# Contracting the first layer of the x tokens over (head, slot) instead of over channels, with M = state @ w_in built on the chip and all stages pipelined anew

## The chip, the cores and the metric

The kernel runs on one core of one Trainium2 chip. The time is the device time of one execution in microseconds (us). A profile is a trace of one execution; its span is about 1.8 us shorter than the time of the same execution.

The engines are called as the profile calls them: PE is TensorE (PEld its weight loads, which overlap its matmuls), DVE is VectorE, ACT is ScalarE, POOL is GpSimd, SP is SyncE. PEclk is the TensorE clock that the profile reports as granted (1.00 is full). The kernels' tiles lie in two on-chip memories: every matmul here writes a PSUM tile, and all other tiles are in SBUF.

## The reference, cut to what matters

Two blocks follow each other. The first is a cross attention in both directions between 512 tokens and 32 state slots for each of 8 batches and 8 heads of 64 channels. The second is a feed-forward block over all 4352 resulting tokens (8 x 512 "x tokens" and 8 x 32 "state tokens").

```python
B, H, S, Ns, D = 8, 8, 512, 32, 64          # d_model = H*D = 512, d_ff = 2048
# attention, per batch and head (scores are scaled by 1/sqrt(D))
a      = softmax(x @ state.T)               # 512 x 32: over the slots
xread  = a @ state                          # 512 x 64
a2     = softmax(state @ x.T)               # 32 x 512: over the tokens
sread  = a2 @ x                             # 32 x 64
t = concat([xread, sread]) over tokens, heads side by side   # (B*544) x 512
# feed-forward
h = t @ w_in                                # 512 -> 2048
g = s * relu(h)**2 + b                      # s and b are single numbers
out = g @ w_out                             # 2048 -> 512
```

The change rests on one identity. For the x tokens, h = sum over the heads of (a_head @ state_head) @ w_in_head = sum over the heads of a_head @ (state_head @ w_in_head). The bracket is M. The left form contracts over 512 channels, and the right form over 8 heads x 32 slots = 256.

## The kernel before

Almost all that PE reads is in fp16. In the transposed layout a batch is a 128x512 tile for every 128 rows of the contraction. The attention builds U = xread.T from the attention weights (`a4`, with 4 heads x 32 slots on the partitions). ACT casts U to the fp16 tiles `XB`, which the first layer reads:

```python
def attn_phase2b(b, ctx):                    # a4 = E * (1 / its sum over slots)
    for g in range(NG):                      # 2 groups of 4 heads
        RBG = ps_tile([P, S], FP32, ...)
        mm(RBG, ind16, R4h_g[g], tp=(0, 0))  # spread the reciprocals by a matmul
        nc.vector.tensor_mul(a4, E4_g[g], RBG)

def attn_phase2cd(b, ctx):
    ...                                      # sread of the batch into srdT (V)
    for g in range(NG):
        for pp in range(2):
            for m in range(2):               # U: contraction over 32 slots
                mm(U[64*m:64*m+64, :], stN[32*hp:32*hp+32, :],
                   a4[32*hp:32*hp+32, :], tp=(32*hp, 64*m))
            nc.scalar.copy(xb, U)            # xb is XB: 4 tiles of 128 channels

def moe_mm1(rhs_tiles, ntok, tag, frange):
    for f in frange:                         # 16 chunks of 128 of d_ff
        for k in range(NKM):                 # 4 matmuls: 512 channels
            nc.tensor.matmul(hps, w_in16[k][:, P*f:P*f+P], rhs_tiles[k], ...)
        nc.scalar.activation(r16, hps, AF.Relu)
        nc.vector.tensor_mul(gt, r16, r16)

def moe_mm2(gts, ntok, out_aps, tag):
    for rr in range(ntok // P):
        for f in range(NKF):                 # 16 matmuls: 2048
            nc.tensor.matmul(ops, gts[f][:, P*rr:P*rr+P], w_out16[f], ...)
        nc.vector.scalar_tensor_tensor(osb, ops, s_bc, bias_bc, ALU.mult, ALU.add)
        nc.sync.dma_start(out_aps[rr], osb)

for b in range(B):
    ...                                      # loads for b + 1
    ctx_b = attn_phase1_2a(b)
    if b > 0: gts_prev = moe_mm1(XB of b-1, chunks 0..7)
    if b == 1: ...                           # 16 matmuls: column sums of w_out, for b
    attn_phase2b(b, ctx_b)
    if b > 0: gts_prev += moe_mm1(XB of b-1, chunks 8..15)
    attn_phase2cd(b, ctx_b)
    if b > 0: moe_mm2(gts_prev, ...)         # all four token groups in a row
```

The second layer is applied to relu(h)^2 alone; s and b come in at the eviction, where `bias_bc` is b times the column sums of w_out.

The softmax here doesn't subtract the row's maximum and nothing guards it: scores larger than these inputs give would overflow.

## Time and profile before

| | before |
|---|---|
| time, median of 4 runs | 319.28 us (319.2 to 320.52) |
| profiled span | 317.4 us |
| PE busy | 297.0 us, 94% |
| DVE, ACT busy | 41%, 35% |
| length of one steady batch | 33.94 us |

The page of the kernel before begins with the busy time of each engine, its share and its number of instructions. Its second part shows tenths of PE's time in 40 equal slices, and its fourth the shares of the chain of work that ended last.

```profile
span 317.4 us, 4788 instructions
PE 297.0 (94%) x1889; PEld 137.8 (43%) x1889; DVE 130.7 (41%) x348; ACT 110.2 (35%) x209; POOL 71.8 (23%) x114
PE   1698799999999999999999999999999999999990
...
PE 87%; DMA 5%; POOL 5%; issue 0%; DVE 0%; POOLq 0%
```

PE works without a visible gap from the sixth slice to the last but one. An average could hide a stage with another limit, so look at stretches of one batch. In the windows of the kernel before, the columns are the stretch and its length, then the busy time and number of instructions of each engine.

```profile
core 0: us, PE busy (x) PEld busy (x) DVE busy (x) ACT busy (x) POOL busy (x), PEclk, DMA share, GB/s
65.30:99.24 33.94, 33.94 (x224) 15.52 (x222) 15.27 (x43) 12.88 (x24) 7.57 (x12) 1.00 0.36 49
167.10:201.00 33.90, 33.90 (x224) 15.50 (x222) 15.22 (x42) 12.88 (x24) 7.36 (x11) 1.00 0.37 50
```

In a steady batch PE is busy for the whole stretch, and the two engines after it less than half of it. Only PE work counts there. What that work is, the chain of waits of the kernel before shows (start, length, what):

```profile
72.41 0.86 PE hps_x_4_924 L282 x4
...
84.04 0.33 PE U_0_0_1080 L67 x2
84.38 0.01 PE U_0_1_1085 L67 x2
84.38 0.21 PE U_1_0_1090 L67 x2
84.59 0.02 PE U_1_1_1095 L67 x2
84.61 3.56 PE ops_x_0_1100 L300 x16
88.17 3.45 PE ops_x_1_1120 L300 x16
```

Four first-layer matmuls take 0.86 us and sixteen second-layer matmuls 3.45 us, so one 128x512 matmul costs 0.216 us of PE, called a slot below. A batch has 64 of each: 128 x 0.216 = 27.6 us. The remaining 6.3 us are attention. The four matmuls of each U group, which use parts of the PE array, cost about one slot together: 0.33 + 0.01 for the first, 0.21 + 0.02 for the second.

### The profile page before, as it was taken

To read this page: it belongs to the slowest core of one execution; us is meant where nothing else is said; L and a number is where in the kernel's file an instruction comes from. 1 tells how busy PE (TensorE), PEld (TensorE's weight loads), DVE (VectorE), ACT (ScalarE), POOL (GpSimd) and SP (SyncE) were. 2 spreads that over 40 slices of the span, in tenths; PEclk is the share of its full clock that TensorE was granted. 3 is DMA by queue.
4 is the path that set the end of the run, shared out by engine and by line. 5 is a ranking of instruction groups with operands and counts; after the bars stand their busy time and mean duration, and the time that the engine had idled before them with its cause. 6 is when DMAs were issued, how large, how long until landed. Compare 5 with 4: busy or idle time off the path is not lost.

```text
span 317.4 us, 4788 instructions
## 1 busy us (share of the span) xinstructions
PE 297.0 (94%) x1889; PEld 137.8 (43%) x1889; DVE 130.7 (41%) x348; ACT 110.2 (35%) x209; POOL 71.8 (23%) x114
## 2 busy tenths in 40 slices
PE   1698799999999999999999999999999999999990
PEld 0343344444444444444444444444444444466440
DVE  0434345156324651266227532564146622554110
ACT  1126223035602561056304650357015620674000
POOL 8728964300350007000800053000000000000000
PEclk9999799999999999999999999999999999999997
DMA  7999993910292009300671039100110001000211
GB/s 47 160 207 188 91 74 26 143 40 1 15 124 72 0 0 98 97 16 0 57 115 37 3 22 114 68 0 2 66 66 3 0 35 66 33 3 0 90 48 63
DMA packets 46489, 18.18 MB, mean 57 GB/s; under 512 B 39554, under 2 KB 41602, under 8 KB 46466
## 3 DMA queue, kind: packets, MB, share of 16 engines
q0 software_dynamic: 41152, 8.92, 31.1%
q1 hardware_dynamic: 5314, 8.95, 8.0%
q8 instruction: 15, 0.25, 0.3%
q14 instruction: 8, 0.07, 0.1%
HBM read 17.86 MB, written 8.91 MB: 84 GB/s over the span
## 4 chain that ended last, share of the span: by engine, by line
PE 87%; DMA 5%; POOL 5%; issue 0%; DVE 0%; POOLq 0%
DMA w_out_0_129<-in_moe_w_out_dram 4%; POOL xn_0_112 L120 2%; PE ops_x_0_693 L300 1%; PE ops_x_0_3121 L300 1%; PE ops_x_0_2728 L300 1%; PE ops_x_0_2321 L300 1%; PE ops_x_0_1100 L300 1%; PE ops_x_0_1914 L300 1%; PE ops_x_0_1507 L300 1%; PE cs_ps L329 1%; DMA stH_1_164<-in_state_dram 1%; PE ops_sr_3589 L300 1%; PE ops_x_2_3529 L300 1%; PE ops_x_0_3489 L300 1%; PE ops_x_3_3181 L300 1%; PE ops_x_1_2748 L300 1%
## 5 line engine op out<-in xcount | busy, mean ns | idle before, releaser
L282 PEld LDWEIGHTS <-w_in_0_121 128*128 128x128 f16 x144 | 14.2, 98 | 16.7 <-issue 4.0
L282 PEld LDWEIGHTS <-w_in_3_127 128*128 128x128 f16 x144 | 14.2, 99 | 14.5 <-issue 1.3
L282 PEld LDWEIGHTS <-w_in_2_125 128*128 128x128 f16 x144 | 14.2, 99 | 12.8 <-issue 0.6
L282 PEld LDWEIGHTS <-w_in_1_123 128*128 128x128 f16 x144 | 14.2, 99 | 12.7 <-issue 1.0
L120 POOL DMA_DIRECT2D xn_6_1999<-in_x_dram x8 | 5.9, 747 | 18.7 <-PE Vps_1_1_1884 L67 18.7
L120 POOL DMA_DIRECT2D xn_7_2406<-in_x_dram x8 | 5.9, 746 | 18.7 <-PE Vps_1_1_2291 L67 18.7
L120 POOL DMA_DIRECT2D xn_4_1185<-in_x_dram x8 | 5.9, 746 | 18.7 <-PE Vps_1_1_1070 L67 18.7
L120 POOL DMA_DIRECT2D xn_5_1592<-in_x_dram x8 | 5.9, 746 | 18.7 <-PE Vps_1_1_1477 L67 18.7
L120 POOL DMA_DIRECT2D xn_3_778<-in_x_dram x8 | 5.9, 746 | 6.8 <-PE Vps_1_1_663 L67 6.7
L120 POOL DMA_DIRECT2D xn_2_349<-in_x_dram x8 | 5.9, 746 | 0.0
L120 POOL DMA_DIRECT2D xn_1_166<-in_x_dram x8 | 5.9, 745 | 0.0
L120 POOL DMA_DIRECT2D xn_0_112<-in_x_dram x8 | 5.9, 745 | 0.0
L290 ACT ACTIVATE r_x_0_2521<-hps_x_0_2516 128x512 f16<-128x512 f32 x1 | 0.6, 598 | 13.7 <-PE hps_x_0_2516 L282 13.7
L290 ACT ACTIVATE r_x_0_1707<-hps_x_0_1702 128x512 f16<-128x512 f32 x1 | 0.6, 598 | 13.7 <-PE hps_x_0_1702 L282 13.7
L290 ACT ACTIVATE r_x_0_1300<-hps_x_0_1295 128x512 f16<-128x512 f32 x1 | 0.6, 597 | 13.7 <-PE hps_x_0_1295 L282 13.7
L290 ACT ACTIVATE r_x_0_2114<-hps_x_0_2109 128x512 f16<-128x512 f32 x1 | 0.6, 597 | 13.7 <-PE hps_x_0_2109 L282 13.7
L290 ACT ACTIVATE r_x_0_2914<-hps_x_0_2909 128x512 f16<-128x512 f32 x1 | 0.6, 597 | 13.7 <-PE hps_x_0_2909 L282 13.7
L67 PE MATMUL stTps_175<-ident_91,stH_0_110 32*128 32x32 f16 x4 | 0.3, 188 | 5.3 <-DMA stH_0_110<-in_state_dram 5.3
L290 ACT ACTIVATE r_x_0_3206<-hps_x_0_3201 128x512 f16<-128x512 f32 x1 | 0.6, 597 | 13.0 <-PE hps_x_0_3201 L282 13.0
L67 PEld LDWEIGHTS <-xn_0_112 128*64 128x64 f16 (+1 forms) x48 | 2.3, 143 | 5.6 <-issue 3.6
L290 ACT ACTIVATE r_x_0_893<-hps_x_0_888 128x512 f16<-128x512 f32 x1 | 0.6, 598 | 12.0 <-PE hps_x_0_888 L282 12.0
L199 ACT ACTIVATE E_0_0_201<-T_0_0_196 128x512 f16<-128x512 f32 x1 | 0.6, 597 | 8.9 <-PE T_0_0_196 L67 8.9
(2153 smaller groups left out, 868.1 us busy)
## 6 DMA issues: line engine op xcount, KB each, us to landing
xn_0_112<-in_x_dram POOLq DMA_DIRECT2D x8, 64.0 KB, 2.9
w_in_0_121<-in_moe_w_in_dram POOLq DMA_DIRECT2D x1, 512.0 KB, 5.4
w_in_1_123<-in_moe_w_in_dram POOLq DMA_DIRECT2D x1, 512.0 KB, 7.4
w_in_2_125<-in_moe_w_in_dram POOLq DMA_DIRECT2D x1, 512.0 KB, 9.3
w_in_3_127<-in_moe_w_in_dram POOLq DMA_DIRECT2D x1, 512.0 KB, 11.2
xn_1_166<-in_x_dram POOLq DMA_DIRECT2D x8, 64.0 KB, 3.0
xn_2_349<-in_x_dram POOLq DMA_DIRECT2D x8, 64.0 KB, 3.2
xn_3_778<-in_x_dram POOLq DMA_DIRECT2D x8, 64.0 KB, 3.6
```

What stands on the lines that cost most here:

```text
L67: return nc.tensor.matmul(out, lhsT, rhs, start=start, stop=stop, tile_position=tp, is_transpose=is_transpose, skip_group_check=skip,)
L120: nc.gpsimd.dma_start(out=xn16[:, :, h, :], in_=x[b, h].rearrange("(q c) d -> q c d", q=P),)
L199: nc.scalar.activation(E4, T4, AF.Exp, scale=scale, accum_out=rs4)
L282: nc.tensor.matmul(hps, w_in16[k][:, P * f : P * f + P], rhs_tiles[k], start=(k == 0), stop=(k == NKM - 1),)
L290: nc.scalar.activation(r16, hps, AF.Relu)
L300: nc.tensor.matmul(ops, gts[f][:, P * rr : P * rr + P], w_out16[f], start=(f == 0), stop=(f == NKF - 1),)
L329: nc.tensor.matmul(cs_ps, ones_col16, w_out16[f], start=(f == 0), stop=(f == NKF - 1))
```

## The change

**Intent.** Per batch, M takes the place of U. M has 256 x 2048 elements, stored with four heads x 32 slots on the partitions, twice. Each of its 4 column chunks needs 8 matmuls (one per head) of 64 rows by 32 columns of the PE array. If those eight run side by side, M costs 4 slots of 0.216 us, and the first layer then needs 32 matmuls instead of 64. The x tokens never exist as such: the first layer reads `a4` and `M`. Along with this the diff changes much else:

- The softmax over slots no longer goes through small reciprocals and a spreading matmul. A block-ones matmul gives the sums on all partitions (D), and ACT makes the reciprocal as exp(-ln D). One table set is loaded ahead for both functions.
- PE's order is written by hand. Stage s interleaves, chunk by chunk, the first layer of batch s, the attention pieces of batch s+1 and the second layer of batch s-2 (`LAG = 2`). The second layers of the last x batch and of the state tokens come at the end.
- The column sums of w_out move from PE to POOL: 15 additions and one fp32 matmul.
- The loads are larger and in another order, and are all issued at the start; 12 matmuls on zeros run on PE at the very start.

The diff, cut to its core:

```diff
-        for g in range(NG):
-            for pp in range(2):
-                U = ps_tile([P, S], FP32, ...)
-                for m in range(2):
-                    mm(U[64*m:64*m+64, :], stN[32*hp:32*hp+32, :], a4[32*hp:32*hp+32, :], tp=(32*hp, 64*m))
-                nc.scalar.copy(xb, U)
+    def head_of(g, q):
+        return 4 * g + (q if g == 0 else q ^ 1)
+    def att_M(b, c):
+        ps = [att_ps([P, FC], FP32, ...) for g in range(NG)]
+        for q in range(4):
+            for g in range(NG):
+                h = head_of(g, q); m = h % 2
+                mm(ps[g][32*q:32*q+32, :],
+                   a["stT"][64*m:64*m+64, g, 32*(h % 4):32*(h % 4)+32],
+                   wi[c][64*m:64*m+64, h // 2, :], tp=(64*m, 32*q))
+        for g in range(NG):                  # cast to fp16: DVE, one in four on ACT
+            ...
+    def att_D(b, g):
+        mm(Dps, bones16, a["E"][g])
+        nc.scalar.activation(L, Dps, AF.Ln)
+        nc.scalar.activation(R, L, AF.Exp, scale=-1.0)
+        nc.vector.tensor_mul(a4, a["E"][g], R)
...
-            for k in range(NKM):             # first layer, 4 matmuls
+            for k in range(n):               # n = 2 for the x tokens: M, a4
...
+        def bias():
+            nc.gpsimd.tensor_tensor(wsum, wof(0), wof(1), ALU.add)
+            for f in range(2, NKF):
+                nc.gpsimd.tensor_tensor(wsum, wsum, wof(f), ALU.add)
+            mm(ps, ones32, wsum)
+            nc.vector.tensor_scalar(bias_bc, ps, b_bc, None, ALU.mult)
+        for _, fn in pieces(0): fn()         # attention of batch 0: the prologue
+        LAG = 2
+        for s in range(B + 1):
+            for f in range(NKF):
+                mm1_f(s, ...)                # s = B: the state tokens, w_in as before
+                ...                          # pieces of attention of batch s + 1
+                if s == LAG and f == 3: bias()
+                if s >= LAG: mm2_part(s - LAG, *divmod(f, 4) ...)   # 4 matmuls
+        ...                                  # second layers of batch 7 and state tokens
```

`head_of` orders the heads of the second group so that the two groups use the two row halves of the array at the same time: the eight matmuls then sit on eight different tiles.

## The prediction

> **What bounds the kernel now.** TensorE. The page gives PE busy 94% of the 317.4 us span, and the chain of waits is 87% PE. In the windows by stage, each of the stretches of one batch (33.9 us) shows PE busy 33.9 of 33.9, DVE 15.2, ACT 12.9, clock 1.00. The chain shows a 128x512 matmul every 0.216 us (0.86 us for four, 3.45 us for sixteen). So one batch is 64 matmuls of the first layer (13.8 us), 64 of the second (13.8 us) and about 6.3 us of attention. Outside the steady batches: first mm1 at 20.0 us, a DMA wait of 3.1 us at 30.6, w_out column sums on PE (3.5 us), and 7.7 us after the last matmul's end.
>
> **What the change removes.** First layer contracts over two groups of 128 (head, slot) instead of four of 128 channels: 32 matmuls fewer per batch, 6.9 us. The U product and its four ACT casts, the DT/R4/RBG matmuls and their small DVE work go; so do the column sums.
>
> **What it adds, per batch.** M: 4 chunks of 8 matmuls, 64 rows x 32 columns x 512. T is packed likewise. Whether eight such tiles run side by side decides the size. The timeline shows the four U tiles (32x64) starting within 10 ns and the next four 0.24 us later: four at once. The T pair takes one slot. The Trainium skill, "TensorEngine Tiling (Array Packing)", Key Properties, says tiles operate independently and that a mode switch drains; the trace agrees on both for the tiles it has (about 0.09 us extra at each entry and exit). Same rows, different columns is not shown clearly by this trace. If all eight overlap: M 4 x 0.25, T 0.25, D 0.43, transposes of x about 1.0, aT 0.46, V 0.5, state 0.1, and about eight islands x 0.19 of switches = 5.3 us; batch = 6.9 + 13.8 + 5.3 = 26.0 us. If only row halves overlap: about 30 us. I take 26.8.
> DVE per batch, from durations read here (osb 0.75, r*r 0.43, f32 PSUM evictions about 0.6 estimated): about 17.5 us; ACT (0.60 each, 0.49 apart when back to back): 24 plus accumulator reads, about 14 us. Both stay below PE, so they cost nothing in steady stages.
>
> **Total (estimate).** Prologue: weights land about 2.45 us per MB of source here (w_in at 14.4, 16.9, 19.4, 21.8); with the chunked order the last w_in chunk comes near 20.5, so stage 0 starts near 21.5. Stages 0 and 1 have no second layer: ACT and DVE bound, about 15 us each. Bias now waits for fifteen POOL additions after all loads and an fp32 matmul: 3 us. Six full stages 6 x 26.8 = 161. Stage 8 (mm2 + state tokens' first layer) 20.8, final second layers 20.8, tail 7.7. Sum 265; the timed median is 2 us over the profiled span: 267.
>
> **On the critical path.** Nearly all of the PE saving in the six full stages (7 us each, 43 us); the two early stages give less.
>
> **What would show it.** First-layer groups of two matmuls, 0.43 us; M's eight matmuls within 0.25 us (right) or about 0.86 us (wrong) in the timeline; steady stages PE over 95% busy, period 26 to 28; stages 0 and 1 with PE well under 100% and ACT near 90%; a PE wait at the bias matmul below 4 us.
>
> **What would make it wrong.** Eight tiles not overlapping (to 290); the fixed PE order making PE wait for DVE in the pieces (aT waits for a2, V for aT's copy); table switches between Ln and Exp; POOL additions blocking DVE or finishing late; loads late.
>
> Chances: faster 0.96, same 0.03, slower 0.01. Predicted 267, range 255 to 288.

## The result, and the profile after

The changed kernel took 269.24 us (median of 4 runs, 268.38 to 270.25), against 319.28 us of the kernel before. The ratio is 0.8425, with a 95% interval of 0.8399 to 0.8451. All ratios here are the mean time of one kernel's fast runs over that of the kernel before's fast runs of the same rounds, so they are not quite the ratio of the medians quoted.

The page after, the same lines as before:

```profile
span 267.3 us, 4515 instructions
PE 239.7 (90%) x1822; PEld 108.6 (41%) x1822; DVE 152.5 (57%) x317; ACT 116.1 (43%) x225; POOL 33.4 (12%) x37
PE   7455944999999999999999999999999999999970
...
PE 79%; DVE 7%; DMA 6%; POOL 2%; ACT 2%; issue 1%; ACTq 0%; POOLq 0%
```

PE lost 57.3 us of work, but the span lost 50.1. The row of slices shows where PE now has gaps: in the first seven slices. The windows of the kernel after, cut at the first matmul of each stage's first layer, name them (columns as before):

```profile
0.00:25.37 25.37, 14.55 (x131) 5.95 (x131) 8.37 (x18) 6.18 (x11) 13.38 (x20) 0.70 1.16 161
25.37:50.83 25.46, 17.76 (x154) 7.41 (x151) 23.61 (x32) 12.73 (x25) 20.02 (x17) 0.77 1.25 184
50.83:65.71 14.88, 14.04 (x151) 5.71 (x150) 13.69 (x34) 12.43 (x26) 0.00 (x0) 0.99 0.01 2
65.71:92.67 26.96, 26.96 (x218) 11.96 (x216) 17.20 (x39) 14.43 (x28) 0.00 (x0) 1.00 0.08 30
...
118.68:144.68 26.00, 26.00 (x215) 11.59 (x214) 16.73 (x38) 13.66 (x26) 0.00 (x0) 1.00 0.11 42
...
196.70:217.42 20.72, 20.72 (x98) 9.41 (x97) 9.46 (x21) 9.56 (x16) 0.00 (x0) 1.00 0.14 51
217.42:238.38 20.96, 20.96 (x130) 12.61 (x129) 7.99 (x21) 6.14 (x16) 0.00 (x0) 1.00 0.14 51
238.38:267.30 28.92, 20.72 (x96) 9.20 (x94) 5.25 (x7) 0.00 (x0) 0.00 (x0) 0.92 0.19 64
```

The lines are: the prologue, stages 0, 1, 2, one of four equal steady stages (3 to 6), stage 7 (no attention left), stage 8 (the state tokens' first layer), and the last second layers with the tail. A steady stage takes 26.0 us with PE busy for all of it; the batch took 33.9 before. Two matters stand out. Stage 0 takes 25.5 us where stage 1, with the same work for PE, DVE and ACT, takes 14.9, and DVE is busy 23.6 us in it instead of 13.7. And the prologue takes 25.4 us, with PE busy for 14.6.

The step of the prediction that mattered most was whether M's eight matmuls run at once. PE's timeline of the kernel after, in a steady stage (start, length, engine, line, operation, out<-in, shapes):

```profile
128.78 0.38 PE L66 MATMUL h_6_1815<-a_4_1_1481,M_1451 128*128 128x512 f16 x1
129.09 0.39 PE L66 MATMUL Mps_0_0_1823<-wi_109,stT_1687 64*32 64x512 f16 x1
...
129.11 0.39 PE L66 MATMUL Mps_0_1_1824<-wi_109,stT_1687 64*32 64x512 f16 x1
129.43 0.39 PE L66 MATMUL o_1_1791<-wo_125,g_8_1124 128*128 128x512 f16 x1
```

They do: eight start between 129.09 and 129.11 us. From the matmul before to the first of them is 0.31 us instead of 0.216, and from the last to the matmul after 0.32, so entering and leaving the tiled mode costs about 0.1 us each time. The Trainium skill, "TensorEngine Tiling (Array Packing)", Key Properties, says that tiles operate independently and that a change of tiling mode drains the engine. This trace agrees with both.

Why is DVE busy in stage 0? DVE's timeline of the kernel after shows instructions of the same shapes in stage 0 (first four lines) and in stage 1 (last three):

```profile
33.04 1.05 DVE L249 TENSOR_SCALAR a_1_0_508<-E_0_416,q_0_506 128x512 f16<-128x512 f16 x1
38.16 1.37 DVE L302 TENSOR_TENSOR g_6_449<-r_6_447 128x512 f16<-128x512 f16 x1
39.46 1.37 DVE L302 TENSOR_TENSOR g_7_469<-r_7_467 128x512 f16<-128x512 f16 x1
40.75 0.68 DVE L240 CAST M_451<-Mps_1_0_486 128x512 f16<-128x512 f32 x1
...
55.98 0.35 DVE L249 TENSOR_SCALAR a_2_0_799<-E_0_707,q_0_797 128x512 f16<-128x512 f16 x1
58.12 0.68 DVE L240 CAST M_742<-Mps_0_1_744 128x512 f16<-128x512 f32 x1
59.17 0.42 DVE L302 TENSOR_TENSOR g_6_740<-r_6_738 128x512 f16<-128x512 f16 x1
```

The square of r, both of whose inputs are read from SBUF, takes 1.37 us instead of 0.42 (others in stage 0 take 0.41 to 1.77). The scaling of E for a2, which reads one SBUF tensor and one number per partition, is delayed as well, 1.05 us instead of 0.35, and so is a4 = E x R (0.77 and 1.37 instead of 0.42). The cast of M, read from PSUM, takes 0.68 in both. In stage 0, and only there, POOL runs the 15 additions for the column sums; its timeline in the same stretch of the kernel after:

```profile
35.25 4.00 POOL L350 TENSOR_TENSOR wsum<-wsum,wo_123 128x512 f32<-128x512 f32 x3
39.33 3.80 POOL L350 TENSOR_TENSOR wsum<-wsum,wo_125 128x512 f32<-128x512 f32 x3
```

The delay reaches PE: in stage 0 PE waits 7.3 us for DVE in all. The two longest waits are for casts of M behind delayed squares (us in total, times, longest):

```profile
PE Mps_1_0_486 L66 <- DVE M_451 L240: 2.4, 1, 2.4
PE Mps_3_1_558 L66 <- DVE M_451 L240: 2.2, 1, 2.2
```

The Trainium skill, "SBUF — State Buffer", Who interferes with whom, says that a DVE instruction with two SBUF inputs contends with a GpSimd instruction that reads SBUF, that (of DVE's two-port modes) whoever issues first holds the shared ports "for the whole instruction", and that instructions with one SBUF input outside the two-port modes do not contend. The square and the cast fit this; whether the scaling for a2 ran in a two-port mode, no view shows. That made it the first suspect; the trace alone does not prove it, because w_out is loaded and PE's clock is lower in the same stage.

### The profile page after: what moved, and what is told of

The parts are those of the page before. It is cut to its first block, busy times and chain, and to the rows that moved or that the text cites. A ratio compares the mean times of both kernels' runs of the same rounds, so it can differ in the third digit from the quotient of the medians.

```text
span 267.3 us, 4515 instructions
## 1 busy us (share of the span) xinstructions
PE 239.7 (90%) x1822; PEld 108.6 (41%) x1822; DVE 152.5 (57%) x317; ACT 116.1 (43%) x225; POOL 33.4 (12%) x37
## 4 chain that ended last, share of the span: by engine, by line
PE 79%; DVE 7%; DMA 6%; POOL 2%; ACT 2%; issue 1%; ACTq 0%; POOLq 0%
DMA wi_117<-in_moe_w_in_dram 6%; PE o_0_2079 L66 1%; PE o_0_1708 L66 1%; PE o_0_2450 L66 1%; PE o_0_1337 L66 1%; PE o_3_1971 L66 1%; PE o_0_948 L66 1%; PE o_3_2713 L66 1%; PE o_2_2622 L66 1%; PE o_3_2342 L66 1%; PE o_2_2251 L66 1%; PE o_2_1880 L66 1%; PE o_3_1600 L66 1%; PE o_2_1509 L66 1%; PE o_3_1229 L66 1%; PE o_2_1138 L66 1%
## 5 line engine op out<-in xcount | busy, mean ns | idle before, releaser
L66 PE MATMUL warm_ps<-warm 128*128 128x512 f16 x12 | 5.3, 632 | 1.2 <-DVE warm L81 1.2
L204 ACT ACTIVATE E_0_209<-T_0_199 128x512 f16<-128x512 f32 x1 | 0.6, 597 | 11.4 <-PE T_1_200 L66 11.4
L66 PEld LDWEIGHTS <-stT_345 64*32 64x32 f16 x40 | 1.1, 91 | 10.6 <-issue 10.2
L350 POOL TENSOR_TENSOR wsum<-wsum,wo_123 128x512 f32<-128x512 f32 x4 | 5.0, 1250 | 0.3
L350 POOL TENSOR_TENSOR wsum<-wsum,wo_125 128x512 f32<-128x512 f32 x4 | 4.9, 1216 | 0.3
L350 POOL TENSOR_TENSOR wsum<-wsum,wo_127 128x512 f32<-128x512 f32 x4 | 4.8, 1199 | 0.3
L66 PEld LDWEIGHTS <-M_1451 128*128 128x128 f16 x32 | 3.1, 98 | 3.8
L66 PEld LDWEIGHTS <-M_1822 128*128 128x128 f16 x32 | 3.1, 98 | 3.8
L66 PEld LDWEIGHTS <-M_1080 128*128 128x128 f16 x32 | 3.1, 98 | 3.8
L66 PEld LDWEIGHTS <-M_2193 128*128 128x128 f16 x32 | 3.1, 98 | 3.8
L66 PEld LDWEIGHTS <-M_742 128*128 128x128 f16 x32 | 3.1, 98 | 3.8
L66 PEld LDWEIGHTS <-M_2564 128*128 128x128 f16 x32 | 3.1, 98 | 3.8
L66 PEld LDWEIGHTS <-stT_159 64*32 64x32 f16 x40 | 0.9, 97 | 9.0 <-DMA wi_115<-in_moe_w_in_dram 3.1
L66 PEld LDWEIGHTS <-M_223 128*128 128x128 f16 x32 | 2.6, 107 | 4.1 <-issue 2.7
L66 PEld LDWEIGHTS <-M_451 128*128 128x128 f16 x32 | 2.5, 101 | 3.8 <-issue 2.3
L66 PEld LDWEIGHTS <-st_104 128*64 128x64 f16 x32 | 1.2, 112 | 6.3 <-issue 3.5
L238 ACT CAST M_223<-Mps_3_1_288 128x512 f16<-128x512 f32 x1 | 0.6, 586 | 6.5 <-PE Mps_3_1_288 L66 6.5
L66 PEld LDWEIGHTS <-warm 128*128 128x128 f16 x12 | 1.6, 144 | 3.9 <-issue 2.8
L66 PEld LDWEIGHTS <-xn_106 128*64 128x64 f16 x64 | 2.2, 147 | 2.4 <-DMA xn_106<-in_x_dram 2.0
L66 PE MATMUL Mps_2_0_275<-wi_115,stT_159 64*32 64x512 f16 x4 | 0.6, 604 | 2.9 <-DMA wi_115<-in_moe_w_in_dram 2.9
L66 PE MATMUL Mps_1_0_486<-wi_111,stT_345 64*32 64x512 f16 x4 | 1.0, 548 | 2.4 <-DVE M_451 L240 2.4
## 6 DMA issues: line engine op xcount, KB each, us to landing
wi_115<-in_moe_w_in_dram POOLq DMA_DIRECT2D x1, 512.0 KB, 14.8
wi_117<-in_moe_w_in_dram POOLq DMA_DIRECT2D x1, 512.0 KB, 16.7
```

The source lines that it names most:

```text
L66: return nc.tensor.matmul(out, lhsT, rhs, start=start, stop=stop, tile_position=tp, is_transpose=is_transpose, skip_group_check=True,)
L204: nc.scalar.activation(E, T[g], AF.Exp, scale=scale, accum_out=rs)
L238: nc.scalar.copy(dst, ps[g])
L350: nc.gpsimd.tensor_tensor(wsum, wsum, wof(f), ALU.add)
```

## The experiments

The questions were: what makes stage 0 long, what share of the gain M has, which property of the tiles it needs, and what the other added parts are worth. Every run gave a correct result, with 4 runs each; the kernel before measured 319.60 to 319.75 us beside them. Each edit is against the kernel after, or on top of another run where that is said. "Stage" times run from first relu to first relu.

| run | us, median | ratio to before | prologue | stage 0 | stage 1 | stage 2 | steady |
|---|---|---|---|---|---|---|---|
| after | 269.24 | 0.8425 | 26.4 | 25.2 | 14.8 | 26.9 | 26.01 |
| e1_pe_bias | 262.61 | 0.8206 | 26.2 | 15.4 | 14.7 | 29.4 | 26.01 |
| e2_pool_twice | 293.56 | 0.9186 | 26.7 | 48.7 | 14.7 | 26.9 | 26.01 |
| e5_two_chains | 275.57 | 0.8623 | 26.3 | 32.0 | 14.7 | 26.9 | 26.01 |
| e3_same_tile | 275.15 | 0.8601 | 26.7 | 25.6 | 15.2 | 27.9 | 27.07 |
| e10_xT_by_half | 269.86 | 0.8439 | 26.9 | 25.5 | 15.0 | 26.9 | 26.06 |
| e4_U_route | 304.46 | 0.9524 | 21.8 | 23.7 | 18.4 | 33.2 | 32.22 |
| e8_no_preload | 294.83 | 0.9230 | 29.5 | 27.4 | 23.1 | 30.2 | 28.73 |
| e12_no_preload_a4_late | 292.45 | 0.9151 | 29.7 | 24.9 | 23.0 | 29.6 | 28.15 |
| e7_no_warm | 269.60 | 0.8440 | 26.0 | 26.3 | 14.9 | 26.9 | 26.01 |
| e6_load_order | 260.52 | 0.8147 | 23.8 | 16.5 | 14.7 | 29.4 | 26.01 |
| e9_best | 256.92 | 0.8038 | 24.0 | 15.3 | 29.4 | 26.0 | 26.01 |
| e11_prologue | 254.67 | 0.7981 | 19.7 | 17.7 | 29.4 | 26.0 | 26.01 |

(In the last two the second layer starts one stage earlier, so stage 1 is already a full one. The cuts here lie at the first relu itself, about a microsecond after those of the windows above at the start, which is why prologue and stage 0 differ a little from those.)

### e1_pe_bias: the column sums on PE

Theory A: POOL's additions hold DVE back. Rival: the loads of w_out, or PE's lower clock, make stage 0 long. The edit takes away POOL's additions and leaves the loads.

```diff
-            nc.gpsimd.tensor_tensor(wsum, wof(0), wof(1), ALU.add)
-            for f in range(2, NKF):
-                nc.gpsimd.tensor_tensor(wsum, wsum, wof(f), ALU.add)
-            mm(ps, ones32, wsum)
+            for f in range(NKF):
+                mm(ps, ones16, wof(f), start=(f == 0), stop=(f == NKF - 1))
```

> One edit to the kernel after: the column sums of w_out for the bias are made by sixteen 128x512 fp16 matmuls on TensorE at the same place (stage 2) instead of fifteen additions on POOL. Theory A (the POOL additions hold up every VectorE instruction that reads SBUF[...]; TensorE then waits for M's eviction): stage 0 falls from 25.5 us to about 15 us, the r*r multiplications take 0.43 us there as elsewhere, stage 2 grows by about 2.5 us (16 x 0.216 less the 0.97 us of the fp32 matmul); total 269 -> about 261. Rival B (stage 0 is long because of the clock of 0.77, PSUM buffers or the loads still running): stage 0 stays near 25 us, total 269 -> about 272.

Measured: 262.61 us, ratio 0.8206 (0.8176 to 0.8236). The windows of this kernel at stages 0 and 2, and one square of stage 0 in DVE's timeline:

```profile
26.17:41.61 15.44, 14.61 (x158) 6.22 (x160) 13.34 (x32) 12.56 (x26) 1.75 (x2) 0.95 1.33 203
...
56.27:85.62 29.35, 29.35 (x234) 13.05 (x230) 17.85 (x40) 13.68 (x27) 0.00 (x0) 1.00 0.08 28
...
32.01 0.42 DVE L301 TENSOR_TENSOR g<-r 128x512 f16<-128x512 f16 x1
```

Stage 0 fell from 25.2 to 15.4 us, and DVE's busy time in it from 23.6 to 13.3, with the loads still running (203 GB/s); the squares take 0.42 us again, and PE waits 0.4 us for DVE. So it was not the loads. The clock rose along with this (0.77 to 0.95), so this run alone doesn't separate it. The trace of the kernel after does: from 28 to 37 us its PEclk is 1.00, and two squares in that stretch took 1.77 and 1.37 us. The rival falls. Stage 2 grew by 2.5 us, as the sixteen matmuls cost more PE time than the one fp32 matmul. Moving "free" work to an idle engine had cost 9.8 us in stage 0 to save 2.5 in stage 2 (by the profiled executions; the medians differ by 6.6 us in all).

### e2_pool_twice: twice the additions on POOL

The opposite direction: a second, useless chain of 15 additions on POOL.

```diff
+            junk = konst.tile([P, DM], FP32, name="junk")
+            nc.gpsimd.tensor_tensor(junk, wof(0), wof(1), ALU.add)
+            for f in range(2, NKF):
+                nc.gpsimd.tensor_tensor(junk, junk, wof(f), ALU.add)
```

> The kernel after with the same POOL additions made a second time into a buffer nobody reads, right after the first: POOL is busy about 49 to 69 us, when the loads have landed. Theory A: stage 1 (14.9 us in the kernel after) stretches to 20 us or more, with r*r at about 1.3 us there; total +5 to +10 us. Rival B (loads or clock made stage 0 long): stage 1 stays at 15 us and the total at 269.

Measured: 293.56 us, ratio 0.9186 (0.9148 to 0.9224): 24 us longer than the kernel after, not a few. The expected place was wrong too: the delay fell in stage 0 (48.7 us), not in stage 1, which stayed at 14.7. The two chains had been interleaved in POOL's order. DVE's timeline of this kernel shows one square that takes 32.67 us:

```profile
31.42 32.67 DVE L302 TENSOR_TENSOR g<-r 128x512 f16<-128x512 f16 x1 [0.83 <-ACT r L300]
```

So this confirmed the cause but not the mechanism as expected: the delay did not grow with the number of additions but jumped. In the kernel after each addition needs the result of the one before, and DVE got a turn between two of them (the additions start 1.3 us apart and take 1.2). Here two independent chains alternate, POOL has the next addition ready at once, and DVE got no turn until they were over. Theory A2: what counts is whether POOL's stream has pauses. The next run tests it with the original number of additions.

### e5_two_chains: as many additions, in two independent chains

```diff
+            nc.gpsimd.tensor_tensor(wsum2, wof(2), wof(3), ALU.add)
-            for f in range(2, NKF):
+            for f in range(4, NKF, 2):
                 nc.gpsimd.tensor_tensor(wsum, wsum, wof(f), ALU.add)
+                nc.gpsimd.tensor_tensor(wsum2, wsum2, wof(f + 1), ALU.add)
+            nc.gpsimd.tensor_tensor(wsum, wsum, wsum2, ALU.add)
```

> The kernel after with its fifteen POOL additions split into two independent chains of running sums that are added at the end: the same number of additions, but neighbours no longer depend on each other, so POOL runs them back to back. From the run with doubled additions (one r*r held for 32.7 us) theory A2: VectorE gets the port only in the gaps that a dependency leaves between two POOL instructions; without gaps one r*r is held for about 15 us, POOL finishes sooner (about 16 us instead of 19.3) and yet stage 0 gets longer than 25.2 us, near 31; total +4 to +7 us. Rival B2 (each POOL instruction costs VectorE its own length, whatever the gaps): stage 0 stays at 25 us or falls by 3.

Measured: 275.57 us, ratio 0.8623 (0.8596 to 0.865). POOL's additions followed each other every 1.11 us from 30.25 to 47.2 us, against about one in 1.3 us in the kernel after. DVE's timeline of this kernel:

```profile
30.52 15.59 DVE L302 TENSOR_TENSOR g<-r 128x512 f16<-128x512 f16 x1 [0.45 <-ACT r L300]
...
47.44 0.15 DVE L247 RECIPROCAL q<-rs 128x1 f32<-128x1 f32 x1
```

One square ends at 46.11 us, when the fourteen additions without a pause are over (45.83 us); the next took 1.48 us beside the last addition, which had to wait for both chains, and then DVE goes on at once. Stage 0 took 32.0 us, 6.8 more than in the kernel after, though POOL finished its work earlier than there. A2 holds: in these runs, the fewer pauses POOL's stream of additions had, the worse it was for DVE.

### e3_same_tile: M's heads two to a tile

This and the next run ask what the packing rests on. Here the second group's heads keep their natural order, so the eight matmuls of a set use only four tiles, each twice.

```diff
-        return 4 * g + (q if g == 0 else q ^ 1)
+        return 4 * g + q
```

> The kernel after with the head order of group 1 not swapped, so that of each pair of consecutive 64x32 matmuls both use the same tile of the array. Theory (distinct tiles overlap, same tile does not): each set of eight takes two slots, +0.216 us for T and each of four M chunks: steady stage 26.0 -> about 27.1 us, total +6 to +8 us. Rival (the order inside a set does not matter): no change.

Measured: 275.15 us, ratio 0.8601 (0.8576 to 0.8626). The steady stage grew from 26.01 to 27.07 us. That is 1.06 us for five sets (M's four and T), 0.212 each: a second slot per set. PE's timeline of this kernel gives the set of eight and what follows:

```profile
135.94 0.62 PE L66 MATMUL Mps<-wi,stT 64*32 64x512 f16 x8
136.50 1.04 PE L66 MATMUL o<-wo,g 128*128 128x512 f16 x4
```

The single records of this set start in two groups of four: at 135.940 to 135.960 and at 136.167 to 136.186 us. In program order the two heads of a tile are neighbours, so a strict queue would have paired only matmuls of different tiles that stand side by side and taken five slots. One record shows more: the one that signals the end of the first group's product, seventh in program order, is in the first four, 0.2 us before the second in program order. The Trainium skill, "TensorE: Matmul & The Clock Gate", Part 3, The mechanism, says of packed matmuls that they are "strict FIFO, no reordering". This trace differs: a matmul that waits for its own tile did not hold up later ones on other tiles. (The order in PE's queue is taken from the source. In nine of the 40 sets, all before stage 2, the matmul with the wait for the second group's PSUM tile started second, as in the source, and in the others fifth; so the order of starts was not fixed by the build.)

### e10_xT_by_half: the order of the x transposes

If order among tiles counted, the 16 transposes of an x piece, which alternate between two column halves, would take longer when each half's come in blocks of four.

```diff
-            for c in range(SCH):
-                for m in range(2):
+            for m in range(2):
+                for c in range(SCH):
```

> The kernel after with the sixteen 128x64 transposes of each x half issued by column half (four with the same tile in a row) instead of alternating the two column tiles. Theory (neighbours on different column tiles overlap, same tile does not): the sixteen take about 16 x 0.056 = 0.9 us instead of 0.57 us, steady stage 26.0 -> about 26.7 us, total +4 to +6 us. Rival (columns of one row group never overlap, so the order does not matter): no change.

Measured: 269.86 us, ratio 0.8439 (0.8405 to 0.8473), the interval overlapping that of the kernel after; the steady stage is 26.06. The expected loss of 0.7 us a stage did not come: my expectation was wrong. It fits what e3 showed: the halves overlap whatever the order within so short a run. How far ahead of a blocked matmul others may go, these runs do not tell.

### e4_U_route: the new pipeline with the old first layer

How much of the 50 us is M, and how much everything else? U comes back in the new schedule (`att_U` in place of `att_M`; the casts are shared by ACT and DVE), and the first layer has its four matmuls again. The head order of e3 and another order of T's matmuls belong to this edit too; the expectation counts two slots for T instead of one, so about 0.2 us a batch of what follows is T's.

```diff
-            (6, lambda: att_M(b, 0)), (8, lambda: att_M(b, 1)),
-            (10, lambda: att_M(b, 2)), (12, lambda: att_M(b, 3)),
+            (10, lambda: att_U(b, 0)), (12, lambda: att_U(b, 1)),
...
-                    mm1_f(s, [a["M"][:, g, :] for g in range(NG)], a["a4"], S, f)
+                    mm1_f(s, [w_in_k(k) for k in range(NKM)], a["XB"], S, f)
```

> The pipeline, loads and fixed TensorE order of the kernel after, but with the first layer of before: U = state x a4 (eight 32x64 matmuls), cast to fp16, then four matmuls per 128 hidden units over the channels; no M. It splits the gain in two. Theory: steady stage = 26.0 - 1.6 (M with its mode switches) + 6.9 (32 matmuls) + about 1.0 (U, T in two slots) = 32.3 us against 33.9 of before; total about 305 to 315. So M would be worth most of the 50 us and the pipelining a few us. Rival (the gain comes mostly from the re-pipelining): total below 290.

Measured: 304.46 us, ratio 0.9524 (0.9493 to 0.9556). The steady stage took 32.22 us, with PE busy for all of it. So of 50 us, measured inside the new pipeline, 304.5 - 269.2 = 35 us come from M and 319.3 - 304.5 = 15 from the rest. Per steady batch, M gives 32.22 - 26.01 = 6.2 us and the rest 33.94 - 32.22 = 1.7. This version starts stage 0 earlier (21.8 us), since its prologue does not wait for w_in.

### e8_no_preload: without the table set loaded ahead

Ln and Exp are used in turn. The preload names a table set that has both. The Trainium skill, "ScalarE: Activation LUTs", Table sets: the hidden batching unit, lists one such set. Without the line a load is placed before each change.

```diff
-    nc.scalar.preload_act_table_set("natural_log_exp_and_others")
```

> The kernel after without the preload of the table set that holds both exp and ln: the build shows 32 more ACT instructions, table loads of 1.28 us each (as the one at the start of both kernels), about four per batch. Theory (TensorE alone bounds the steady stages, ACT has 13.7 of 26.0 us busy): steady stages stay at 26.0 us with ACT busy about 19; only stage 1, where ACT is the fullest engine, stretches from 14.8 to 18 to 20 us; total +3 to +6 us. Rival (the chain Ln, Exp, a4 is on the critical path): steady stages lengthen, total +20 us or more.

Measured: 294.83 us, ratio 0.923 (0.9189 to 0.9272). The loss is 25.6 us, where I had expected 3 to 6 from the early stages alone. The groups by line of this kernel show 32 loads beside the one at the start that the kernel after has too, 16 at the Ln (below: busy time, mean ns, idle time before) and as many at the reciprocal:

```profile
L212 ACT ACT_TABLE_LOAD x16 | 20.5, 1283 | 0.3
```

DVE's and PE's timeline of this kernel shows what they do to a steady stage, which became 28.73 us long:

```profile
123.03 0.42 DVE L216 TENSOR_TENSOR a<-E,R 128x512 f16<-128x512 f16 x1 [3.42 <-ACT R L214]
...
124.11 0.37 PE L66 MATMUL Mps<-wi,stT 64*32 64x512 f16 x1 [0.83 <-DVE M L239]
...
125.04 0.41 PE L66 MATMUL Mps<-wi,stT 64*32 64x512 f16 x7 [0.56 <-DVE M L239]
```

ACT has time to spare in a steady stage (13.7 of 26.0 us busy without the loads, and four loads of 1.28 are 5.1 more). But a4 waited 3.42 us at the head of DVE's queue for the reciprocal R, the cast of M stood behind it, and PE's fixed order waited for that cast. Latency, not load, lengthened the stage. My expectation had counted ACT's load only. The same page, What ACT_TABLE_LOAD costs, gives 1283 ns for a load, as here, and about 2.66 us for a whole switch; here a relu ended at 119.15 us and the Ln behind the next load began at 120.46, so the whole switch took 1.31 us.

### e12_no_preload_a4_late: the same, with a4 moved behind the casts of M

If DVE's queue, blocked at a4, were the whole mechanism, moving a4 behind the last cast of M in DVE's order should give back nearly all.

```diff
+            with tc.issue_after(a["cast"].ins):      # the last cast of M
+                nc.vector.tensor_mul(a4, a["E"][g], a["R"][g])
```

> Run e8 (no preload; steady stages grew from 26.0 to 28.7 us although ACT was busy only 19 of them) with the two multiplications a4 = E x R put behind the last eviction of M in VectorE's order. Theory: in e8 VectorE sat 3.4 and 1.9 us at a4 for R, and M's evictions, for which TensorE waits, stood behind it in the same in-order queue; with a4 late the steady stages return to 26.0 to 26.4 us and the total falls from 295 to about 278 (the prologue and stages 0 and 1 stay long). Rival (the table loads delay relu or M's ACT copies themselves): steady stages stay above 28 us.

Measured: 292.45 us, ratio 0.9151 (0.9121 to 0.9182); the steady stage is 28.15 us. Only 0.6 of the 2.7 us came back, so my theory covered the smaller part. DVE's and PE's timelines of this kernel show the same wait in another place:

```profile
120.60 0.43 DVE L308 TENSOR_TENSOR g<-r 128x512 f16<-128x512 f16 x1 [2.40 <-ACT r L306]
...
121.68 0.41 PE L66 MATMUL Mps<-wi,stT 64*32 64x512 f16 x7 [1.01 <-DVE M L245]
```

DVE now waits 2.40 us for the relu, which stands behind table loads and R in ACT's queue. The cast of M stands behind that square, and PE behind the cast. In a steady stage PE waits 1.0 us there, and another 0.7 us directly for ACT's own cast of M. So the rival explanation, that the relus and ACT's casts themselves are late, fits 1.7 of the 2.1 us that stayed; no run takes these two away to prove it. Both queues pass the delay on in order.

### e7_no_warm: without the 12 matmuls on zeros

```diff
-        wps = att_ps([P, 512], FP32, "warm_ps")
-        for _ in range(12):
-            mm(wps, warm[:, 0:P], warm)
```

> The kernel after without its twelve warm-up matmuls (1.2 to 6.5 us in its trace). In that trace TensorE then waits 1.8 us for the state and the T matmuls at 12.8 us still take the slow 0.60 us, and the prologue ends with the wait for the last w_in chunk. Theory: the warm-up bought nothing; total unchanged at 269 within 1 us. Rival: a colder clock in the prologue and stage 0, +1 to +3 us.

Measured: 269.6 us, ratio 0.844 (0.8414 to 0.8465): no difference. In the kernel after these matmuls end at 6.5 us, and PE then waits 1.82 us for the state's load. The matmuls of T at 12.8 us still take 0.60 us each, where those at 71.6 us take 0.39. Without them T's matmuls take 0.62 us. The warm-up bought nothing here; whether one without the pause after it would, is open.

### e6_load_order: w_in before the second x

On top of e1. The last chunk of w_in ended the prologue, and x of batch 1 was loaded before it. This is in the chain of waits of the kernel after (start, length, what):

```profile
7.12 16.67 DMA wi_117<-in_moe_w_in_dram
```

```diff
     load_wi(0)
     load_wi(1)
-    load_x(1)
     load_wi(2)
     load_wi(3)
+    load_x(1)
```

> The kernel of run e1 (column sums on TensorE) with x of batch 1 loaded after the last two chunks of w_in instead of before. Theory: the wait for the last w_in chunk ends the prologue, at one load of 1 MB of source per about 2.5 us; the first relu comes at 23.7 instead of 26.2 us and the total falls from 262.6 to about 260. Rival (batch 1 then waits for its x, or the order does not matter): total unchanged at 262 to 263.

Measured: 260.52 us, ratio 0.8147 (0.8124 to 0.817), 2.1 us less than e1. The first relu came 2.4 us earlier (23.8 us), and stage 0 took 1.1 more (16.5 us). PE waits only 0.3 us of that for x of batch 1, which now comes later, and in e9 with the same load order stage 0 takes 15.3 us; the rest is not explained. So a wrong place in the load order cost about 2 us of the prologue.

### e9_best: and the second layer one stage earlier

On top of e6, `LAG = 1`. There is one half-empty stage fewer at the start, and one pure second-layer stretch fewer at the end.

```diff
-        LAG = 2
+        LAG = 1
...
-        for rr in range(SCH):
-            mm2_part(B - 1, rr, 0, NKF, x_dst(B - 1, rr))
```

> Run e6 with the second layer one stage behind the first instead of two: column sums and the first second layer move to stage 1, and the last stage loses 13.8 us. Theory: stage 1, which leaves TensorE little idle (14.0 of 14.9 us busy in the kernel after), so only the idle time of stage 1 and some of the mode switches are won: total about 1 us below run e6, near 259. Rival: the shorter lag makes TensorE wait for the last r*r of the stage before: slower than e6.

Measured: 256.92 us, ratio 0.8038 (0.8015 to 0.8062), 3.6 us less than e6 where I had expected about 1. The stage of 14.7 us without a second layer, and the 41.05 us from the first relu of stage 8 to the last matmul became one full stage (26.0 us) and 27.2 us. That is 55.7 against 53.2 us, 2.5 of the 3.6; prologue and stage 0 together took 1.0 less, for which no cause is shown. My expectation was too small because it read PE's 14.0 busy of 14.9 us in that stage as work. At the rate of the steady stages that work is 26.0 - 13.8 = 12.2 us (an estimate: a steady stage less its 64 second-layer matmuls), so the half-empty stage left 2.5 us unused.

### e11_prologue: part of batch 0's attention moved into stage 0

The original load order, PE's column sums, `LAG = 1`; the prologue keeps only what stage 0's first chunks need, and M's chunks 2 and 3 and V of batch 0 move into stage 0.

```diff
+            if s == 0:
+                todo = [(4, lambda: att_M(0, 2)), (7, lambda: att_M(0, 3)),
+                        (11, lambda: att_V(0))] + todo
```

> Column sums on TensorE, second layer one stage behind, loads in the order of the kernel after, and M's last two chunks and V of batch 0 moved into stage 0 so that the first layer starts when two chunks of w_in are there. Theory: the first relu comes at about 19 us instead of 24.0, TensorE's order then meets the last chunk near 24 us without waiting; total 3 to 5 us below run e9 (256.9), 252 to 254. Rival (stage 0 or 1 then waits for loads instead): no gain.

Measured: 254.67 us (254.54 to 255.79), ratio 0.7981 (0.7953 to 0.801). The first relu came at 19.7 us, so stage 0 no longer waits for all of w_in, and takes 17.7 us itself. The gain is slightly less than expected. This version is faster than both kernels: 0.7981 / 0.8425 = 0.947 of the kernel after.

## Why the prediction was right or wrong

The forecast "faster" was right, and 269.24 lies near the 267 predicted. The sum was built as listed in the prediction, so each term can be held against the profile after.

| term | predicted us | measured us | error |
|---|---|---|---|
| prologue to stage 0 | 21.5 | 25.4 | +3.9 |
| stages 0 and 1 | 15 + 15 | 25.5 + 14.9 | +10.3 |
| bias | 3 | 1.0 | -2.0 |
| five full stages (2 to 6) | 5 x 26.8 | 130.0 | -4.0 |
| stage 7 | 26.8 | 20.7 | -6.1 |
| stage 8 | 20.8 | 21.0 | +0.2 |
| last second layers | 20.8 | 20.7 | -0.1 |
| tail | 7.7 | 8.2 | +0.5 |
| sum | 264.6 | 267.3 (the span) | +2.7 |

(The error column is computed before rounding.) The sum is near because the errors cancel, +14.9 against -12.2, and that they cancel is luck. (The prediction rounded its sum to 265, for the span, and added 2 for the time.) The steps were:

1. **"Eight tiles side by side" was right.** M's eight matmuls start within 0.02 us. Its own itemised estimate gave 26.0 us for a batch; the steady stage measured 26.0. The 26.8 used in the sum was a hedge between full and half overlap that the chip did not need. e4 shows that M is worth 6.2 us per steady batch and e3 that a set without distinct tiles costs one more slot of 0.21 us.
2. **"PE stays the limit of the full stages" was right.** DVE's 16.7 us and ACT's 13.7 us a stage are close to the 17.5 and 14 predicted, and PE has no gap. The remaining engines cost nothing there, as said; e8 and e12 show that this rests on their latency as well as on their load.
3. **"Stages 0 and 1 about 15 us each" failed for stage 0.** For stage 1 it was right in size (14.9 us), though not in the sign it named: ACT was to be near 90% busy, and the trace has ACT at 84%, DVE at 92% and PE at 94% (of which 12.2 us are work, see e9). For stage 0, the prediction named POOL's additions blocking DVE as a danger, but gave it no time and no weight in the sum. It cost 25.2 - 15.4 = 9.8 us (e1), and it can be far worse with the additions in another order (e5, e2). That mechanism is shown: taking the additions away removes it, and regrouping them makes it worse, with no other work of the stage changed.
4. **"w_in's last chunk near 20.5" was mis-sized.** The chunk was needed last, and landed at 23.8 us. The prediction took the weight rate from the trace before, and its 20.5 leaves no room for x of batch 1 standing in front (one load is about 2.5 us). e6 shows about 2.4 us of the 3.9 to be that order. The rest is not settled by an experiment.
5. **"Six full stages" miscounted.** Stage 7 has no attention of a next batch, so it is 20.7 us, with only the 96 matmuls of two layers (96 x 0.216 = 20.7). That was readable in the diff. It is the largest error to the other side.
6. **"Bias: 3 us" was mis-sized.** The fp32 matmul took 0.97 us and PE did not wait at all, because POOL was done by 49.5 us, well before stage 2. The price of the POOL route lay in stage 0 instead.

What was expected of the experiments failed in four places: e2 (where and how much), e8 (which counted ACT's load and not the latency), e9 (about 1 us expected, 3.6 measured) and e10; e11 fell just short (252 to 254 expected, 254.67 measured); and e12 showed that the explanation of e8 by DVE's queue alone was only a small part of it. What stays open is the last 0.4 of the 2.1 us in e12, what made stage 0 of e6 longer than that of e9, and how far ahead of a blocked matmul others may start.

## What to carry to other kernels

When a product of three matrices can be bracketed in two ways, cost both in PE slots, and let small matmuls fill distinct tiles of the array: a set of eight cost one slot and about 0.2 us for the switches. Before giving an idle POOL work that reads SBUF, ask which DVE instructions that read SBUF run then (here the squares, a4 and a2 were held up, the casts from PSUM were not), and whether PE needs what stands behind them; sixteen matmuls for 2.5 us were better than fifteen "free" additions. Count the first and last stages of a pipeline one by one, for there the pieces differ: all that the experiments gained after the change lay in them (269.2 to 254.7 us), and none in the steady stages.

## What the Trainium skill lacked or had wrong

- "SBUF — State Buffer", Who interferes with whom, says of DVE's two-port modes that the lock lasts for the whole instruction. The runs show that DVE can be held for much longer: when POOL's instructions follow each other without a pause, DVE does not get a turn between them, and one square of 0.42 us took 15.6 us (e5) or 32.7 us (e2). With each addition waiting for the one before, it mostly took 1.37 us. The page does not tell of this difference.
- "TensorE: Matmul & The Clock Gate", Part 3, The mechanism, states strict FIFO order of matmuls without reordering. In e3 the seventh matmul of a set started 0.2 us before the second, which waited for its tile, and a set cost one more slot (0.21 us), where strict order would have cost four more; in e10 the order of transposes made no difference (26.06 against 26.01 us).
- "ScalarE: Activation LUTs", What ACT_TABLE_LOAD costs, gives about 2.66 us for every switch of set. The load measured 1.28 us, as it says, but from the end of the instruction before to the start of the one after only 1.31 us passed (e8).
- The same page does not tell what a load of 1.28 us on an engine with slack costs elsewhere: 0.8 us per load here (25.6 us for 32 loads), through the in-order queues of ACT and DVE.
